# Backward pass of attention and a gated MLP: P and dS kept in pairs of row tiles, and one transposing DMA a pair

## The chip, the cores and the metric

The kernel runs on one core of a Trainium2 chip. A core has TensorE (PE in the profile; PEld is its weight load), VectorE (DVE), ScalarE (ACT), GpSimd (POOL) and SyncE (SP), an on-chip memory of 128 partitions (SBUF), matmul accumulators (PSUM), and 16 DMA engines that serve all its queues. Here SP issues DMAs on the hardware queue (q1 in the profile), POOL on the software queue (q0). The metric is device time in microseconds (us), the median of several runs.

## What is computed

The reference is a block whose output is `x + s * g`, and the gradients of it for nine outputs. With `xn` the layer norm of `x` (2048 rows, 576 columns):

```python
q = (xn @ wq)                      # 32 heads of 128
p = softmax(q @ k.T * Dh ** -0.5)  # 2048 x 2048 in each head
s = (p @ v) @ wo
h = sigmoid(xn @ w_gate) * (xn @ w_up)   # 4608 columns
g = silu(h @ w_down)
out = x + s * g
```

The kernel returns `out` and the gradients for x, the K and V caches, wq, wo, w_gate, w_up and w_down. K and V are given as caches of 32 heads, 2048 keys, 128 columns; all is bf16. For one head the backward pass needs P and dS = P * (dP - delta), both 2048 x 2048, in two forms: as they are, with queries on partitions, as the moving operand of dV = P^T dO and dK = dS^T Q; and turned, with keys on partitions, as the stationary operand of O = P V and dQ = dS K.

## The kernel before

**Stages.** (1) The gated MLP forward and its row-wise results, to 460 us of the profiled execution. (2) The 32 heads, one after the other with an overlap, 460 to 3670 us. (3) Output rows and the gradient that goes into the MLP (3670 to 3800). (4) A loop over 18 blocks of 256 MLP columns (F blocks) that makes dh, dw_down, dw_up and dw_gate (3800 to 4410). (5) dwo and dwq by groups of four heads (4410 to 4660). (6) dx by blocks of 256 rows (to the end).

**A head.** NT = 16 row tiles of 128 queries. `s_half` (L544) makes half a row of scores (two matmuls of 512 columns) and DVE scales it and takes its running minimum; `s_exp` (L558) makes the row tile P(q) of 128 x 2048 on ACT; `dp_half` (L573) makes dP and, on DVE and ACT, the row tile dS(q). Each P(q) and dS(q) is a buffer of 512 KB in the pool `slab` (20 buffers). `trans_dma` (L599) issues from SP a transposing DMA that turns one row tile into 16 blocks of 128 x 128 in the pool `wpt` (7 buffers). One row tile, dS(9), is turned on PE instead (`trans_pe`, L602, over `pe_transposes`, L515: eight 128 x 128 transposes into a PSUM bank, then a copy by ACT or DVE, twice). `rows` and `row_mm` (L608) then multiply the turned tile by V or K, 16 matmuls of 128 columns a row tile, four row tiles to an accumulator; `o_sink` (L650) and `dq_sink` (L670) take the results away. `kv` and `kv_mm` (L626, L635) make dV and dK from the slabs as they are, in two passes each (VA, VB, KA, KB), and store them transposed (dvT_d, dkT_d).

**Order.** PE, DVE and ACT run the heads in an order written out by hand: each piece of work has a position, 64 a head, and the program is sorted by it (`at`, `anchor`, L442). Scores of row tile q stand at 2q and 2q + 1, dP at 32 + 2q and on; O starts at `XO`, dQ at 32 + `XQ`; the matmuls of dV and dK fill from `KV0` to `KV1`, spread by `level` so that each position holds the same load. Work of the next head (Q, K, V preparations) has positions in this one. SP and POOL are not in that order: a scheduler sets theirs, and each runs in order once it is set. SP issues all transposes of a head. A transpose waits for its row tile and for its `wpt` buffer.

**Turning back.** dvT_d and dkT_d have to be turned into the output's form: 64 transposes of 512 KB (HBM to SBUF, `turn`, L151) and 64 writes, all on SP. `turn(pool, n)` first writes what the call before loaded, then loads n more. It is called once in each F block (n = 2, 36 in all), once a group in stage 5 (n = 2, 16 in all) and in stage 6 (n = 1, the last 12). In an F block SP also loads the a and b blocks of the block after next (`load_abh`, L878) and a piece of w_down, turned (`load_wdT`, L836). SP's order in stages 3 to 6 is that of the program text.

## Time and profile before

| | us |
|---|---|
| median of 3 runs (lowest, highest) | 5088.66 (5080.39, 5103.23) |
| profiled execution: its time, its span | 5100.3, 5098.5 |
| PE busy in the span | 4977.9 (98%) |
| DVE, ACT, POOL busy | 3087.7, 2435.7, 1484.0 |
| heads, stage 2 | 460 to 3670 |
| granted PE clock (mean) | 0.994 |
| P turned by DMA: 512, median from issue to landing | 5.8 |
| dS turned by DMA: 480, median from issue to landing | 5.9 |

The page gives busy time by engine, a timeline in 40 slices, the DMA queues with the share of the span that their packets took, the chain of work that ended last, and the costliest groups of instructions with the idle time before them and what ended it. SPq is SP's own queue: a DMA's duration there is the time that SP was held by its issue, waits included, and not the time to its landing. As packets overlap, the shares of the queues can sum to over 100%. A matmul's duration holds its way through the array; back to back, a 128-column one starts every 0.056 us.

### The profile page before, as it was taken

How to read it: one execution, taken by the hardware profiler on the slowest of the kernel's cores; microseconds unless marked ns; L12 is line 12 of the kernel's file. 1: busy time of each engine (PE TensorE's matmuls, PEld its weight loads, DVE VectorE, ACT ScalarE, POOL GpSimd, SP SyncE). 2: the span in 40 equal slices, each digit the busy share in tenths (PEclk: the TensorE clock that was granted, in tenths of full speed). 3: DMA queues.
4: the chain of work that ended last, by engine and by line, in shares of the span. 5: the costliest groups of instructions: out<-in, count | busy, mean ns of one | idle time of the engine just before them, and what ended most of it. 6: DMA issues, size and time to landing. Idle time of an engine off the chain costs nothing.

```text
span 5098.5 us, 103815 instructions
## 1 busy us (share of the span) xinstructions
PE 4977.9 (98%) x43024; PEld 3071.8 (60%) x43024; DVE 3087.7 (61%) x4821; ACT 2435.7 (48%) x3131; POOL 1484.0 (29%) x2197
## 2 busy tenths in 40 slices
PE   9999999999999999999999999999899999899999
PEld 3344666666666666666666666666457777654554
DVE  6556778878887887887888788777432222110101
ACT  5533656666666676666666667666202122100000
POOL 4322323333333333233333323322223223211000
PEclk9999999999999999999999999999999999999999
DMA  7889999999999999999999999999999999999995
GB/s 260 265 206 167 197 198 201 198 197 200 202 200 203 203 201 204 202 203 202 199 200 200 205 204 197 199 199 203 189 235 262 230 244 252 282 278 254 207 198 119
DMA packets 2855051, 1079.04 MB, mean 212 GB/s; under 512 B 2659889, under 2 KB 2782769, under 8 KB 2854577
## 3 DMA queue, kind: packets, MB, share of 16 engines
q1 hardware_dynamic: 2769312, 786.61, 87.3%
q0 software_dynamic: 85264, 285.79, 19.8%
q8 instruction: 336, 5.51, 0.4%
q14 instruction: 139, 1.13, 0.1%
HBM read 172.54 MB, written 234.55 MB: 80 GB/s over the span
## 4 chain that ended last, share of the span: by engine, by line
PE 86%; DMA 8%; issue 2%; DVE 2%; ACT 1%; POOL 1%; SPq 0%; DVEq 0%; POOLq 0%; ACTq 0%
PE acc L612 16%; PE acckv L630 15%; PE sp L552 8%; PE acc L1072 8%; PE dp L582 7%; PE accp L511 5%; PE accw L947 4%; DMA dST<-dSq 4%; PE dh L905 3%; PE acc L392 3%; PE accd L923 3%; PE acc L1005 3%; PE acc L852 2%; PE accq L1014 2%; PE acct L518 2%
## 5 line engine op out<-in xcount | busy, mean ns | idle before, releaser
L563 ACT ACTIVATE Pq<-sneg,nm 128x2048 bf16<-128x2048 bf16 x512 | 1025.0, 2002 | 182.6 <-DVE sneg L554 181.6
L585 DVE SCALAR_TENSOR_TENSOR dSq<-dp,delta,Pq 128x1024 bf16<-128x1024 f32 x608 | 774.9, 1282 | 445.9 <-PE dp L582 442.9
L612 PE MATMUL acc<-Kn,dST 128*128 128x128 bf16 x8192 | 977.0, 219 | 36.9 <-DMA dST<-dSq 36.2
L612 PEld LDWEIGHTS <-dST 128*128 128x128 bf16 x8192 | 692.3, 98 | 464.7 <-DMA dST<-dSq 57.6
L612 PE MATMUL acc<-Vn,PT 128*128 128x128 bf16 x8192 | 948.8, 219 | 11.7 <-DMA PT<-Pq 11.6
L612 PEld LDWEIGHTS <-PT 128*128 128x128 bf16 x8192 | 682.7, 98 | 428.8 <-DMA PT<-Pq 18.6
L630 PE MATMUL acckv<-Pq,dOn 128*128 128x512 bf16 x2048 | 762.9, 380 | 0.0
L630 PE MATMUL acckv<-dSq,Qn 128*128 128x512 bf16 x2048 | 758.9, 379 | 0.0
L554 DVE TENSOR_SCALAR_CACHE_REDUCE sneg<-sp,nm 128x1024 bf16<-128x1024 f32 x512 | 657.0, 1283 | 97.6 <-PE sp L552 64.8
L554 DVE TENSOR_SCALAR_CACHE_REDUCE sneg<-sp 128x1024 bf16<-128x1024 f32 x512 | 625.2, 1221 | 92.2 <-PE sp L552 82.8
L588 ACT ACTIVATE t<-dp,negdelta 128x1024 bf16<-128x1024 f32 x416 | 464.8, 1117 | 426.0 <-PE dp L582 324.5
L552 PE MATMUL sp<-KT,QT 128*128 128x512 bf16 x2048 | 610.5, 380 | 7.3 <-DVE sneg L554 7.0
L582 PE MATMUL dp<-VT,dOT 128*128 128x512 bf16 x2048 | 609.9, 379 | 0.6 <-DVE dSq L585 0.5
L592 DVE TENSOR_TENSOR dSq<-t,Pq 128x1024 bf16<-128x1024 bf16 x416 | 307.3, 739 | 0.0
L571 POOL TENSOR_TENSOR dOn<-dOn,rinv_all 128x256 bf16<-128x256 bf16 x256 | 153.8, 610 | 491.6 <-DVE dOn L42 305.4
L630 PEld LDWEIGHTS <-dOn 128*128 128x128 bf16 x2048 | 200.5, 98 | 74.5 <-issue 0.4
L630 PEld LDWEIGHTS <-Qn 128*128 128x128 bf16 x2048 | 200.5, 98 | 73.8
L511 PE MATMUL accp<-xnT,wq_h 128*128 128x512 bf16 x640 | 240.9, 381 | 2.8 <-ACT xnT L40 0.8
L947 PEld LDWEIGHTS <-xn_all 128*128 128x128 bf16 x2304 | 224.2, 98 | 27.8
L1085 DVE SCALAR_TENSOR_TENSOR junk<-dxn,xn_all 128x576 f32<-128x576 f32 x16 | 12.1, 758 | 369.3 <-ACT dxn L1080 369.3
L676 POOL DMA_DIRECT2D dq_d<-dq_n x128 | 99.1, 774 | 456.6 <-DVE dq_n L675 419.4
L1072 PEld LDWEIGHTS <-cf 128*128 128x128 bf16 x2304 | 146.3, 98 | 141.3 <-DMA cf<-dg_d 3.8
(186 smaller groups left out, 7059.2 us busy)
## 6 DMA issues: line engine op xcount, KB each, us to landing
out_dram<-turn SPq DMA_DIRECT2D x64, 512.0 KB, 4.9
h_d<-h_row POOLq DMA_DIRECT2D x48, 384.0 KB, 3.0
a_d<-a_row POOLq DMA_DIRECT2D x48, 384.0 KB, 3.5
b_d<-b_row POOLq DMA_DIRECT2D x48, 384.0 KB, 4.5
a_blk<-a_d SPq DMA_DIRECT2D x18, 1024.0 KB, 8.3
b_blk<-b_d SPq DMA_DIRECT2D x18, 1024.0 KB, 21.4
du_d<-du_blk POOLq DMA_DIRECT2D x18, 1024.0 KB, 9.6
dg_d<-dg_blk POOLq DMA_DIRECT2D x18, 1024.0 KB, 12.5
```

The source lines that it names most:

```text
L511: nc.tensor.matmul(acc[:], lhsT=w[:, i, :], rhs=(srcT if i < DL else xnT)[:, i, cs], start=(i == 0), stop=(i == DL))
L552: nc.tensor.matmul(sp[:, c * CH:(c + 1) * CH], lhsT=hs.QT[:, qs], rhs=hs.KT[:, hf * HW_ + c * CH: hf * HW_ + (c + 1) * CH], start=True, st ...
L554: nc.vector.tensor_scalar(sneg[:, hf * HW_:(hf + 1) * HW_], sp[:], -SCALE, None if hf == 0 else nm[:, hf - 1:hf], op0=ALU.mult, op1=ALU.mi ...
L563: nc.scalar.activation(Pq[:], sneg[:], AF.Exp, bias=nm[:, hf:hf + 1], scale=-1.0, accum_out=hs.rs_all[:, qt:qt + 1])
L582: nc.tensor.matmul(dp[:, c * CH:(c + 1) * CH], lhsT=hs.dOT[:, qs], rhs=hs.VT[:, hf * HW_ + c * CH: hf * HW_ + (c + 1) * CH], start=True, s ...
L585: nc.vector.scalar_tensor_tensor(dSq[:, hsl], dp[:], hs.delta[:, qt:qt + 1], Pq[:, hsl], op0=ALU.subtract, op1=ALU.mult)
L588: nc.scalar.activation(t[:], dp[:], AF.Identity, bias=hs.negdelta[:, qt:qt + 1], scale=1.0)
L592: nc.vector.tensor_tensor(dSq[:, hsl], t[:], Pq[:, hsl], op=ALU.mult)
L612: nc.tensor.matmul(bx.acc[:, j, :], lhsT=T[qt][:, kt, :], rhs=getattr(hs, rhs)[:, kt, :], start=(kt == 0), stop=(kt == NT - 1))
L630: nc.tensor.matmul(bx.acc[i][:], lhsT=getattr(hs, rhs)[:, qt, :], rhs=slabs[qt][:, k0:k0 + CH], start=(qt == 0), stop=(qt == NT - 1))
L947: nc.tensor.matmul(acc[:kd, :FB], lhsT=xn_all[:, st, d0:d0 + kd], rhs=blk_[:, st, :], start=(st == 0), stop=(st == NT - 1))
L1072: nc.tensor.matmul(accs[sl][j][:, :nn], lhsT=ch[:, kk, sl * P:(sl + 1) * P], rhs=w_[:, n0:n0 + nn], start=(pi == 0 and kk == 0), stop=(las ...
```

## The change

P and dS of two neighbouring row tiles now lie in one slab buffer (`[P, 2, S]`, 10 buffers), and one transposing DMA from SP turns both into 32 blocks of 128 x 128 (`trans_P`, `trans_dS`; `wpt` has 4 buffers of two row tiles). It is issued after the second row tile. dS(9) goes by DMA as well, and `trans_pe` is gone, with its load in the planner. O and dQ start 1.5 positions later (`XO`, `XQ` 12.1 to 13.6), and the positions of the preparations, of dV and dK are set anew. The scaling of Q by the softmax's denominators is a step of its own (`q_scale`). To fit, `wq_h` and `ou` have one buffer instead of two, and the stores of dV, dK and dQ share three. `turn` loads at most one, before it writes the older ones; it is called 27 times in the F blocks (once in each, and once more at the start of every odd one, with three buffers), 16 in stage 5 (twice a group), 21 in stage 6. In the F blocks `load_wdT` now stands ahead of `load_abh`.

```diff
...
-    def turn(pool, n):
-        while turned:
-            nc.sync.dma_start(*turned.pop(0))
-        for _ in range(n):
-            if turns:
-                src, dst = turns.pop(0)
-                t_ = pool.tile([P, NT, P], bf, name="turn")
-                nc.sync.dma_start_transpose(t_[:], src)
-                turned.append((dst, t_[:]))
+    def turn(pool, load=True):
+        old, turned[:] = list(turned), []
+        if load and turns:
+            src, dst = turns.pop(0)
+            t_ = pool.tile([P, NT, P], bf, name="turn")
+            nc.sync.dma_start_transpose(t_[:], src)
+            turned.append((dst, t_[:]))
+        for (dst, t_) in old:
+            nc.sync.dma_start(dst, t_)
...
     KPC = CH // P
-    NSLAB, NPT = 20, 7
+    NSLAB, NPT = 10, 4
     STT2 = {4, 9, 14}
-    PE_P = set()
-    PE_DS = {9}
     with tc.tile_pool(name="ld2", bufs=2) as ld2, tc.tile_pool(name="ld1q", bufs=1) as ld1q, \
...
                 self.t_ = {}
+                self.Pp = {}
+                self.dSp = {}
                 self.dS = [None] * NT
...
             hc = slice(hs.h * P, (hs.h + 1) * P)
-            hs.wq = wh.tile([P, DT, P], bf, name="wq_h")
+            hs.wq = wh.tile([P, DT, P], bf, name="wq_h", bufs=1)
             nc.gpsimd.dma_start(hs.wq[:, :DL, :], A_wq[:DL * P, hc].rearrange("(t p) c -> p t c", p=P))
...
             pe_transposes(lambda j: hs.QT[:, j * P:(j + 1) * P], hs.Qn, g, eng)
+        def q_scale(hs, g):
             gs = slice(g * 8, (g + 1) * 8)
...
             hf = NHF - 1
-            Pq = slabp.tile([P, S], bf, name="Pq", tag="slab")
-            hs.P[qt] = Pq
-            nc.scalar.activation(Pq[:], sneg[:], AF.Exp, bias=nm[:, hf:hf + 1], scale=-1.0, accum_out=hs.rs_all[:, qt:qt + 1])
+            if qt % 2 == 0:
+                hs.Pp[qt] = slabp.tile([P, 2, S], bf, name="Pq", tag="slab")
+            Pq = hs.P[qt] = hs.Pp[qt - qt % 2][:, qt % 2, :]
+            nc.scalar.activation(Pq, sneg[:], AF.Exp, bias=nm[:, hf:hf + 1], scale=-1.0, accum_out=hs.rs_all[:, qt:qt + 1])
...
             if hf == 0:
-                hs.dS[qt] = slabp.tile([P, S], bf, name="dSq", tag="slab")
+                if qt % 2 == 0:
+                    hs.dSp[qt] = slabp.tile([P, 2, S], bf, name="dSq", tag="slab")
+                hs.dS[qt] = hs.dSp[qt - qt % 2][:, qt % 2, :]
             dSq = hs.dS[qt]
...
-        def t_tile(T, qt, name):
-            if T[qt] is None:
-                T[qt] = wpt.tile([P, NT, P], bf, name=name, tag="PT")
-            return T[qt]
-        def trans_dma(T, slabs, qt, name):
-            nc.sync.dma_start_transpose(t_tile(T, qt, name)[:], slabs[qt][:])
-        def trans_pe(T, slabs, qt, name, g, eng):
-            pe_transposes(lambda j: slabs[qt][:, j * P:(j + 1) * P], t_tile(T, qt, name), g, eng)
+        def trans_dma(T, pair, qt, name):
+            t_ = wpt.tile([P, 2 * NT, P], bf, name=name, tag="PT")
+            nc.sync.dma_start_transpose(t_[:], pair[:].rearrange("p a s -> p (a s)"))
+            for j in range(2):
+                T[qt + j] = t_[:, j * NT:(j + 1) * NT, :]
+        def trans_P(hs, qt):
+            trans_dma(hs.PT, hs.Pp.pop(qt), qt, "PT")
+        def trans_dS(hs, qt):
+            trans_dma(hs.dST, hs.dSp.pop(qt), qt, "dST")
...
                 c = half * 2 + i
-                kv_t = stg.tile([P, CH], bf, name="kv")
+                kv_t = stg.tile([P, CH], bf, name="kv", tag="stg", bufs=3)
                 alt.copy(kv_t[:], acc[:], eng=KVE[i])
...
             def sink(acc):
-                bx.ou = wt.tile([P, GQ, P], bf, name="ou")
+                bx.ou = wt.tile([P, GQ, P], bf, name="ou", bufs=1)
                 alt.copy(bx.ou[:], acc[:], eng=OUE)
...
             def sink(acc):
-                dq_n = stg.tile([P, GQ, P], bf, name="dq_n")
+                dq_n = stg.tile([P, GQ, P], bf, name="dq_n", tag="stg", bufs=3)
                 nc.vector.tensor_tensor(dq_n[:], acc[:], bcast(hs.rsc[:, gs], GQ), op=ALU.mult)
...
         HEAD = 2 * H1
-        XO, XQ = 12.1, 12.1
+        XO, XQ = 13.6, 13.6
         KVE, OUE = "ss", "s"
-        WOT_AT, DST_PE = 2.0, (6.3, 8.2)
-        QT_AT, DOT_AT = ((41.4, 46.7, 50.0, 53.8), "s"), ((5.6, 8.6, 13.4, 17.4), "s")
-        KT_AT, DON_AT, VT_AT, QN_AT = (45.5, 49.2, "s"), (16.2, 25.4, "v"), (29.6, 31.2, "s"), (33.6, 39.4, "s")
+        WOT_AT = 1.6
+        QT_AT, DOT_AT = ((39.0, 47.2, 50.2, 56.4), "s"), ((7.8, 10.4, 16.2, 18.6), "s")
+        KT_AT, DON_AT, VT_AT, QN_AT = (42.0, 43.6, "s"), (14.9, 24.4, "v"), (3.4, 26.4, "s"), (28.0, 32.2, "s")
         PSTEP = 0.4
...
-        KV0, KV1, GAP = 24.0, 86.7, 1.1
+        KV0, KV1, GAP = 23.2, 85.9, 1.1
         BLK, WIDE = 1.0, CH / P
...
             load_[int(p_)] += DT
-        for ps_, n_ in [((KT_AT + DON_AT + VT_AT + QN_AT), 8), ([H1 + 2 * q_ + d_ for q_ in PE_DS for d_ in DST_PE], 8)]:
+        for ps_, n_ in [((KT_AT + DON_AT + VT_AT + QN_AT), 8)]:
             for p_ in ps_:
...
                 if len(out) < n and len(out) % (2 * KPC) == 0:
-                    pos = max(pos, 4.0 * (len(out) // (4 * KPC)) + 8.0)
+                    pos = max(pos, 4.0 * (len(out) // (4 * KPC)) + 7.0)
             return out, pos
...
                 at(b + QN_AT[g], prep_qn, hs, g, QN_AT[2])
+                at(b + max(QN_AT[g] + 0.3, 16 * g + 14.2 + RINV_AT), q_scale, hs, g)
             for p in range(NT // 2):
...
                 at(p1 + EXP_AT, s_exp, hs, qt)
-                if qt in PE_P:
-                    for g in range(2):
-                        at(p1 + 5.3 + g, trans_pe, hs.PT, hs.P, qt, "PT", g, "s")
-                else:
-                    at(p1 + PT_AT, trans_dma, hs.PT, hs.P, qt, "PT")
-                if qt in PE_DS:
-                    for g in range(2):
-                        at(p2 + DST_PE[g], trans_pe, hs.dST, hs.dS, qt, "dST", g, "sv"[g])
-                else:
-                    at(p2 + DST_AT, trans_dma, hs.dST, hs.dS, qt, "dST")
+                if qt % 2:
+                    at(p1 + PT_AT, trans_P, hs, qt - 1)
+                    at(p2 + DST_AT, trans_dS, hs, qt - 1)
             for g in range(NG):
...
         FB = min(256, F)
-        with tc.tile_pool(name="b1o", bufs=2, reuse_waits="tile") as outp, tc.tile_pool(name="b1k", bufs=2, reuse_waits="tile") as tkp, tc.tile_pool(name="b1t", bufs=3, reuse_waits="tile") as tmpp, \
+        with tc.tile_pool(name="b1o", bufs=2, reuse_waits="tile") as outp, tc.tile_pool(name="b1k", bufs=3, reuse_waits="tile") as tkp, tc.tile_pool(name="b1t", bufs=3, reuse_waits="tile") as tmpp, \
                 tc.tile_pool(name="b1r", bufs=2, reuse_waits="tile") as dblk, \
...
             for fb in range(F // FB):
+                if fb % 2:
+                    turn(tkp)
                 fcols = slice(fb * FB, (fb + 1) * FB)
...
                         make_dwd(fl)
-                load_abh(fb + 2)
                 if fb < DT * (NWD - 1):
                     load_wdT(fb % DT, 1 + fb // DT)
-                turn(tkp, 2)
+                load_abh(fb + 2)
+                turn(tkp)
                 for (blk_, out_, nm) in ((du_blk, out_7, "dwu"), (dg_blk, out_6, "dwg")):
...
                     nc.gpsimd.dma_start(out_[D - KL:, fcols], dwl[k * KL:(k + 1) * KL, :])
-            turn(tkp, 0)
+            turn(tkp, False)
         pcw.release()
...
                                              start=(st == 0), stop=(st == NT - 1))
+                    if hl == 0:
+                        turn(tkp)
                     dwo = sb.tile([P, D], bf, name="dwo")
...
                     nc.sync.dma_start_transpose(dst[:, :, d0:d0 + kd], src[d0:d0 + kd, :])
-                turn(tkp, 2)
-            turn(tkp, 0)
+                turn(tkp)
+            turn(tkp, False)
...
                     elif sbi and pi % 3 == 1:
-                        turn(tkp, 1)
+                        turn(tkp)
                     last = pi == len(passes) - 1
...
                     (nc.sync if sbi == NSB - 1 else nc.gpsimd).dma_start(o1[rows, :], dx[:])
-            turn(tkp, 0)
+            turn(tkp, False)
             assert not turns
...
```

## The prediction

> **What bounds the kernel now.** I read the page's first part, then busy time by stage, then who PE waits for, then DMA and SP's queue over one head. Over the span TensorE (PE) is 98% busy and the hardware DMA queue 87%:
> ```profile
> PE 4977.9 (98%) x43024; PEld 3071.8 (60%) x43024; DVE 3087.7 (61%) x4821; ACT 2435.7 (48%) x3131; POOL 1484.0 (29%) x2197
> ...
> q1 hardware_dynamic: 2769312, 786.61, 87.3%
> ```
> Heads 1 to 30 (560 to 3530 us; the second column is the stretch, the third PE's busy time), and what PE waits for there (us in all, times, longest):
> ```profile
> 560.00:3530.00 2970.00, 2941.27 (x26825) 1870.99 (x26823) 2385.27 (x3453) 1944.47 (x2221) 989.78 (x1405) 1.00 1.14 201
> ...
> PE acc L612 <- DMA dST<-dSq: 19.4, 23, 1.9
> PE acc L612 <- DMA PT<-Pq: 3.4, 5, 1.8
> ```
> All but 6 of PE's 29 idle us there are waits for a row tile that a transposing DMA has not turned yet. DVE is 80% busy, ACT 65%: neither bounds. The first score matmul of head 1 starts at 563.98, that of head 31 at 3530.25: 98.9 us a head; a head without a wait takes 97.87 (1557.75 to 1655.62, head 11). Positions below are 64ths of a head, 1.53 us.
>
> One head (1459 to 1557 us) by DMA queue, and SP's own queue over it (start, duration, count):
> ```profile
> q1 hardware_dynamic: 62576, 15.78, 99.4%
> q0 software_dynamic: 1161, 3.39, 13.1%
> ...
> 1467.34 50.15 SPq L600 DMA_TRANSPOSE PT<-Pq  x16
> 1517.59 44.45 SPq L600 DMA_TRANSPOSE dST<-dSq  x13
> ```
> The reader is to see that SP issues one transpose behind the other without a gap: 16 in 50.15 us, 3.13 each, while PE makes a row tile every two positions (3.06). In this head P(7) is ready at 27.1 us from its first score matmul, its transpose begins at 31.8 and lands at 36.7, PE uses it at 40.2. So the transposing queue is a second bound, level with PE. Taking plain traffic off at its own share (13.1% of 97.9 = 12.8 us), 31 transposes share 85.1 us: 2.74 each.
>
> After the heads PE loses time in a few gaps (3800 to 4430 us):
> ```profile
> PE acc L1005 <- DMA onb<-on_d: 13.0, 1, 13.0
> PE dh L905 <- ACT dhc L909: 8.6, 3, 7.7
> PE dh L905 <- DMA wdT<-in_B_w_down_dram: 7.9, 1, 7.9
> ```
>
> **The change part by part.** The sum is made against the profiled execution: 5100.3 us (span 5098.5), 11.6 above the median of the three runs, 5088.66.
>
> *Removed: PE's turning of dS(9).* 16 transposes a head, 512 in all. In the chain eight take 0.45 us, 0.056 each:
> ```profile
> 1498.24 0.45 PE acct L518 x8
> ```
> 512 x 0.056 = 28.8 us, on the engine that is 99% busy: **-28.8**, and an undisturbed head becomes 97.0. With them go 32 evictions on ACT (1.00 us) and 32 on DVE (0.68); both engines have over 19% idle: 0.
>
> *Added and merged: DMA transposes.* 31 a head of 512 KB become 16 of 1 MB; the bytes turned rise by 1/31. The trace has no 1 MB transpose out of SBUF. The nearest row has the same size, queue and engines, but reads HBM (last stage, two of them):
> ```profile
> 4959.69 9.61 SPq L1061 DMA_TRANSPOSE cq<-dq_d  x2
> ```
> 4.8 us each. The other end is two singles, 2 x 2.74 = 5.48. A head's DMA time would be 12.8 + 16 x 4.8 = 89.6, or 12.8 + 16 x 5.48 = 100.5; PE's 97.0 is reached at 5.26 a pair. I take 5.0 (nearer to the row of the same size, with some surcharge for plain traffic that stops a longer DMA as well): 92.8, so PE sets the head and the queue gets 4 us of slack that it hasn't now. By that most waits go; I keep 9 of the 22.8 us, since longer DMAs come in coarser steps: **-14**. Ends: no wait left, -23; a DMA-bound head of 100.5, (100.5 - 98.9) x 31 = +50 in place of -28.8 and -14.
>
> [...] The rows first: a cf transpose (24 blocks of 128x128) takes 3.4 us on SP's queue, cq (32) 4.8, wqT (8) 1.3: 0.14 to 0.16 a block at any length. [...]
>
> *Later and coarser.* A pair goes out when its second tile is ready. P(7) was ready 27.1 us after the start, 3.7 positions behind its slot (14), so pair k is ready at 4k + 5.7 and O uses it from 4k + 13.6: 7.9 positions, 12.1 us. A 1 MB transpose lands 7.3 us after issue (cq's median), so a backlog of 4.8 us is borne; before it was 8.4 positions, 12.8 us, less 5.8 = 7.0. dS has some 9 positions, 13.7 us, less 7.3 = 6.4. The margin is thinner; that it holds hangs on the queue's slack. If it is gone, PE stands still with kv, score and dP matmuls behind it in its written order, and DVE and ACT wait in turn.
>
> *Buffers.* Four pairs of turned tiles for seven singles: pair k+4 is wanted at 4k + 20.7, buffer k is free at 4k + 17.6, 3 positions before (2.6 before the change). Slabs: from the written positions the tightest are dS pair 2, wanted at 40.0, freed by the second dV pass at 38.3 (dS(4) had 1.3 positions): 0. One wq buffer: free when Q's projection ends at 58.0, next read at 39.0 a head later: its load waits in POOL's queue, behind it dq writes that nobody waits for soon: 0. One ou, three shared stg tiles: at most three are written together (dV's last two and a dQ, near 53): 0 to +3 in all, taken 0.
>
> *Retuned positions* (Q, dO, K, V preparations, dV/dK from 23.2 to 85.9): same instructions, PE work moved inside a head: 0, ends -5 and +10, seen only where a head has no fill. Splitting q_scale off moves POOL work (1.9 us each) that POOL, 33% busy, hides.
>
> *Head 31 and the tail.* SP's order keeps an oT transpose ahead of the last dS. Now:
> ```profile
> 3652.19 7.48 SPq L600 DMA_TRANSPOSE dST<-dSq  x1
> ```
> PE waits 12.7 us for it. Then the last pair waits there: one more tile to turn (2.4) and 16 more matmuls after it (0.9): **+3**, ends 0 and +6.
>
> *turn().* In the F-block loop SP carried two turns per block and waited 109 us for their writes, since a turn needs a buffer whose write was issued just ahead. Now 27 turns (not 36), three buffers, the transpose ahead of the older write, wdT ahead of the a/b loads. The 7.9 us for wdT should go: it was issued at 3982, behind two turns of 13 and 17 us, and now leaves a block earlier. The 7.7 us (b_blk landed 3 us after the loop wanted it) should mostly go, but wdT's 8 to 18 us on SP now stand ahead of the a/b loads: **-11**, ends -15.6 and +8. The 13 us at the next stage end with onb, whose issue waits for PE's last accw of the loop: **-2** (less traffic beside it), ends -6 and +2. Nine more turns go to the last stage, where the DMA share is 0.62 in the last 148 us: hidden. But the last one's write now stands behind the last dx write on SP (5095.6); a turn's write lands 2.8 to 4.9 us after issue, dx's landed 1.8 after: **+2**, ends +1 and +4.
>
> Sum: -28.8 - 14 + 3 - 11 - 2 + 2 = -50.8: 5049 in an execution like the profiled one; less 11.6, **5038** as a median, said 5040.
>
> **The rivals.**
> 1. *Pairs cost as much as two singles, and the transposing queue bounds the head (slower).* One mechanism: at more than 5.26 us a pair 16 pairs and plain traffic pass PE's 97.0; at 5.48 a head takes 100.5. For it: SP's queue never stands still now, a 32nd tile is added, the price looks like one per block. Against: cq's 4.8, and between two singles there is a new start of the queue each time. Heads +50, the rest -8: 5088.7 + 42 = 5131. It ends slower from about 5.4 a pair on.
> 2. *The queue stays level with PE* (5.2 to 5.35 a pair): the 28.8 us are given back as waits at L612; heads -5, the rest -8: 5076, inside the half per cent.
> 3. *All waits go*: pairs at 4.8, no stall, both loop gaps closed: -28.8 - 23 + 1 - 15.6 - 6 + 1 = -71: 5017. For it: 8 us of slack a head.
>
> **How the numbers follow.** Half a per cent (25 us) is about what a measurement of this kernel can tell from no change: the three runs before span 23 us. Chances: forecast 0.46, rival 3 0.20, rival 2 0.15, rival 1 0.19. Faster by over 0.5% (under 5063): 0.66; within: 0.15; slower: 0.19. The forecast's own range with rival 3 is 5005 to 5062; to leave out no more than 2 in 10 it has to reach into rival 1: 5005 to 5125, as the DMA's price is open from both sides.
>
> **What would show it.** Right: dST and PT about 5 us each on SP's queue with gaps between them, so that SP waits for data; PE's period near 97.0 a head; waits at L612 under 10 us in heads 1 to 30; no acct from dSq; no wait for wdT. Wrong: SP's queue again without gaps and 16 pairs in over 84 us, waits for dST in the hundreds of ns in every head (rival 2) or 2 us and more (rival 1); a new wait of dh for b_blk; DVE or ACT waiting for slabs; a longer end than 3 us behind the last dx.

## The result, and the profile after

The changed kernel takes 5139.77 us (median of 11 runs; 5112.70 to 5157.23) against 5102.59 us for the kernel before, run beside it. The ratio is 1.0065, with a 95% interval of 1.0038 to 1.0091: slower by 0.65%, where the forecast was 5040 us and faster. The profiled execution spans 5154.8 us, 56.3 more than the one of before.

Stage by stage, in the two profiled executions (each stage runs from its first instruction to the next stage's first; the heads are counted from each head's first exponential on ACT):

| stage | before, us | after, us | difference |
|---|---|---|---|
| up to head 1 | 568.8 | 578.6 | +9.8, of which 9.3 lie before the first score matmul (470.1 to 479.4) |
| heads 1 to 30 | 2966.3 | 2996.0 | +29.7 |
| head 31 and the last dQ | 135.0 | 128.0 | -7.0 |
| output rows | 131.4 | 142.1 | +10.7 |
| F blocks, with the wait before dw | 621.0 | 621.9 | +0.9 |
| dw | 253.4 | 258.1 | +4.7 |
| dx | 422.6 | 429.9 | +7.3 |

Two of these differences should not be read as the change's alone: the first and the output rows. Three of the kernels below (e1_lag8, m_turnold, g4_qs) are the same as the changed one up to the first score matmul and start it at 468 to 469 us; the granted clock up to head 1 was 0.985 to 0.988 in them and 0.979 here. The output rows take 135.8 to 146.6 us in the twelve profiles with pairs and 131.4, 135.7 and 137.8 in the three with singles, so the kernel before had the shortest of all; what the change adds there was not taken apart. The profiled execution of the changed kernel (5156.55 us) is also one of its slowest: by the medians the loss is 37 us and not 56.

In the heads PE's work did shrink: an average head took 98.88 us with 0.80 of PE waits before, and 99.87 with 2.66 after, so 98.08 and 97.21 without them. The waits took it back. First, who PE waits for in heads 1 to 30 of the changed kernel (us in all, times, longest):

```profile
PE acckv L635 <- POOL dOn L573: 22.2, 30, 0.8
PE acckv L635 <- ACT kv L40: 21.4, 30, 0.7
PE acc L617 <- ACT dOT L40: 15.0, 30, 0.8
PE acct L517 <- ACT VT L40: 11.7, 30, 0.5
PE acc L617 <- DMA dST<-dSq: 5.8, 4, 3.2
```

The reader is to see the column of counts. The waits for turned tiles, 22.8 us before, are down to 5.8 in 4 places. Four others stand 30 times each, once in every head, at the same place (a fifth, for KT's copy, 30 times 0.12 us, lies below what this view lists). A wait that occurs in every head at the same place points to the written order and not to chance on the queue; the experiments test that.

SyncE's queue over head 11 (start, duration, count) holds 8 pairs in 48.69 us, 6.09 each with the waits for their data in it, where the forecast had 5 us each and gaps between them.

```profile
1582.22 48.69 SPq L600 DMA_TRANSPOSE PT<-Pq  x8
1631.01 44.00 SPq L600 DMA_TRANSPOSE dST<-dSq  x7
```

What has changed is how far it runs behind: before, a transpose began on average 1.6 to 8.4 us after its tile was ready (by the tile's place in the head), now 0.1 to 2.0 us.

After the heads, the wait for wdT and the 13.0 us for onb are gone, and in their place stand five for dhc, ACT's copy of dh (3840 to 4480 us):

```profile
PE dh L906 <- ACT dhc L910: 22.7, 5, 9.7
PE accd L924 <- DMA h_blk<-h_d: 3.1, 1, 3.1
```

How one of these comes about is seen on SyncE's queue (start, duration; PE's wait of 8.1 us ends at 3967.7):

```profile
3921.15 16.67 SPq L156 DMA_TRANSPOSE turn<-dvT_d  x1
3939.18 0.36 SPq L159 DMA_DIRECT2D out_dram<-turn  x1
3939.59 2.18 SPq L836 DMA_TRANSPOSE wdT<-in_B_w_down_dram  x1
3941.86 0.56 SPq L884 DMA_DIRECT2D a_blk<-a_d  x1
3942.51 14.70 SPq L884 DMA_DIRECT2D b_blk<-b_d  x1
```

The turn holds the queue 16.67 us, a_blk can only be issued at 3941.86 and lands at 3962.48, b_blk at 3966.40; VectorE's products with them (du_blk waits 8.1 us for a_blk, then dg_blk 3.5 for b_blk) hold dhc, and dhc holds PE. The chain that ended last is 68% "DMA b_blk<-b_d" over the 35 us from 3940 to 3975.

### The profile page after: what moved, and what is told of

Read it like the earlier page. It is cut to its first block, busy times and chain, and to the rows that moved or that the text cites. A ratio compares the mean times of both kernels' runs of the same rounds, so it can differ in the third digit from the quotient of the medians.

```text
span 5154.8 us, 100626 instructions
## 1 busy us (share of the span) xinstructions
PE 4926.1 (96%) x41765; PEld 3051.4 (59%) x42512; DVE 3157.1 (61%) x4789; ACT 2415.2 (47%) x3099; POOL 1479.5 (29%) x2197
## 3 DMA queue, kind: packets, MB, share of 16 engines
q14 instruction: 127, 1.04, 0.1%
## 4 chain that ended last, share of the span: by engine, by line
PE 76%; DMA 7%; issue 6%; DVE 5%; ACT 5%; POOL 1%; SPq 1%; ACTq 0%; DVEq 0%; POOLq 0%; another core or an unknown queue 0%
PE acc L617 14%; PE acckv L635 13%; PE acc L1075 8%; PE dp L586 7%; PE sp L553 6%; PE accp L510 5%; PE accw L948 4%; DVE sneg L555 3%; PE acc L391 3%; PE dh L906 2%; PE accd L924 2%; PE acc L1006 2%; PE accq L1017 2%; DMA b_blk<-b_d 2%; PE acc L851 2%
## 5 line engine op out<-in xcount | busy, mean ns | idle before, releaser
L617 PE MATMUL acc<-Kn,dST 128*128 128x128 bf16 x8192 | 1034.5, 219 | 28.3 <-DMA dST<-dSq 16.7
L589 DVE SCALAR_TENSOR_TENSOR dSq<-dp,delta,Pq 128x1024 bf16<-128x1024 f32 x608 | 773.2, 1281 | 378.8 <-PE dp L586 377.2
L617 PEld LDWEIGHTS <-dST 128*128 128x128 bf16 x8192 | 713.8, 98 | 466.8 <-issue 28.0
L635 PE MATMUL acckv<-dSq,Qn 128*128 128x512 bf16 x1915 | 707.5, 380 | 23.1 <-ACT kv L40 22.1
L635 PE MATMUL acckv<-Pq,dOn 128*128 128x512 bf16 x1892 | 701.0, 380 | 26.5 <-POOL dOn L573 22.8
L553 PE MATMUL sp<-KT,QT 128*128 128x512 bf16 x1985 | 597.9, 380 | 7.0 <-DVE sneg L555 6.7
L586 PE MATMUL dp<-VT,dOT 128*128 128x512 bf16 x1913 | 580.4, 379 | 1.8 <-DVE dSq L589 1.0
L596 DVE TENSOR_TENSOR dSq<-t,Pq 128x1024 bf16<-128x1024 bf16 x416 | 407.4, 979 | 0.0
L1088 DVE SCALAR_TENSOR_TENSOR junk<-dxn,xn_all 128x576 f32<-128x576 f32 x16 | 12.1, 758 | 381.3 <-ACT dxn L1083 381.3
L1083 ACT ACTIVATE dxn<-acc 128x512 f32<-128x512 f32 (+1 forms) x32 | 12.8, 406 | 413.6 <-issue 344.3
## 6 DMA issues: line engine op xcount, KB each, us to landing
dg_d<-dg_blk POOLq DMA_DIRECT2D x18, 1024.0 KB, 12.8
```

The source lines that it names most:

```text
L553: nc.tensor.matmul(sp[:, c * CH:(c + 1) * CH], lhsT=hs.QT[:, qs], rhs=hs.KT[:, hf * HW_ + c * CH: hf * HW_ + (c + 1) * CH], start=True, st ...
L586: nc.tensor.matmul(dp[:, c * CH:(c + 1) * CH], lhsT=hs.dOT[:, qs], rhs=hs.VT[:, hf * HW_ + c * CH: hf * HW_ + (c + 1) * CH], start=True, s ...
L589: nc.vector.scalar_tensor_tensor(dSq[:, hsl], dp[:], hs.delta[:, qt:qt + 1], Pq[:, hsl], op0=ALU.subtract, op1=ALU.mult)
L596: nc.vector.tensor_tensor(dSq[:, hsl], t[:], Pq[:, hsl], op=ALU.mult)
L617: nc.tensor.matmul(bx.acc[:, j, :], lhsT=T[qt][:, kt, :], rhs=getattr(hs, rhs)[:, kt, :], start=(kt == 0), stop=(kt == NT - 1))
L635: nc.tensor.matmul(bx.acc[i][:], lhsT=getattr(hs, rhs)[:, qt, :], rhs=slabs[qt][:, k0:k0 + CH], start=(qt == 0), stop=(qt == NT - 1))
```

## The experiments

The theory that the traces suggested: the pairs do what was forecast, and the loss is made by the retuned positions (the waits above, some 2.5 us a head). Rival A: the pairs themselves cost it. Rival B: the turn part makes it. Each kernel below was run beside the kernel before on the same chip, and its ratio is to that.

### One constant of the planner put back (e1_lag8)

```
-                    pos = max(pos, 4.0 * (len(out) // (4 * KPC)) + 7.0)
+                    pos = max(pos, 4.0 * (len(out) // (4 * KPC)) + 8.0)
```

> The changed kernel with the planner's floor put back from 7.0 to 8.0 and nothing else. Theory (the retuned positions cost: VA's last row tiles now come ahead of the last dOn scaling, 0.74 us of PE wait in each of the 30 heads, 22.2 us of the 79.7 us that PE waits there): the wait of accumulation VA for dOn goes, but VB then lets go of the first pair of P later and the slab of dS pair 2 comes later, so a new wait of the dP/dS work may take part of it: heads 1 to 30 fall by 0 to 22 us, total 5110 to 5140 us. Rival A (pairs themselves cost, positions do not): the wait only changes its name, heads stay at 99.9 us each. Rival B (the turn part costs): unchanged within noise.

Measured: 5124.34 us, ratio 1.0050 (1.0021 to 1.0079). Heads 1 to 30: 2975.8 us, 20.2 less than the changed kernel. PE's waits there:

```profile
PE dp L586 <- ACT t L592: 16.6, 30, 0.6
PE acc L617 <- DMA dST<-dSq: 14.2, 11, 3.0
PE dp L586 <- DVE dSq L589: 9.1, 30, 0.5
```

The wait for dOn is gone, and so, by the shift of everything behind it, are those for the copies of kv and dOT. A new one has come, 0.85 us a head of the dP products: with a floor of 8.0 the second dV pass lets go of the first pair of P 0.7 positions after dS pair 2 wants that slab (worked out from the written positions; 1.7 ahead with 7.0). So 7.0 bought the slab in time, and paid with dOn. The place of the new wait fits that; no run isolates it. The heads fell within the theory's 0 to 22 us; the timed gain alone, 1.0065 to 1.0050, is inside the intervals.

### All positions of before, the later rows kept (e2_oldpos)

```
-        QT_AT, DOT_AT = ((39.0, 47.2, 50.2, 56.4), "s"), ((7.8, 10.4, 16.2, 18.6), "s")
+        QT_AT, DOT_AT = ((41.4, 46.7, 50.0, 53.8), "s"), ((5.6, 8.6, 13.4, 17.4), "s")
...
-        KV0, KV1, GAP = 23.2, 85.9, 1.1
+        KV0, KV1, GAP = 24.0, 86.7, 1.1
```

> The changed kernel with all of the positions of before (weights, QT, dOT, KT, dOn, VT, Qn, start of KV streams, floor 8.0); pairs, the later O and dQ rows and the turn part stay. Theory (positions cost about 2.5 us a head): the five waits that stand in every head (dOn 0.74, kv copy 0.71, dOT copy 0.50, VT copy 0.39, KT copy 0.12 us) go, heads 1 to 30 at about 97.5 us each instead of 99.87, so 60 to 75 us less: about 5070 us; if the slab of dS pair 2 is then waited for, 0.5 to 1 us of it comes back per head. Rival A (pairs cost the time): heads stay at 99 to 100 us, total 5120 to 5150 us. Rival B (turn part): heads may fall, the stages behind the heads keep the 10 us more of the output rows.

Measured: 5353.67 us, ratio 1.0510 (1.0449 to 1.0571). A plain miss: 106.44 us a head, not 97.5. Waits in heads 1 to 30:

```profile
PE accp L510 <- DVE dq_n L680: 54.3, 30, 1.8
PE acckv L635 <- ACT kv L40: 51.5, 30, 1.7
PE acckv L635 <- POOL dOn L573: 46.3, 30, 1.5
PE acc L617 <- DVE dq_n L680: 40.0, 30, 1.3
```

Again each stands in every head (another, for ou's copy, 38.8 us, twice), and most are for evictions. Projections, turnings, O and dQ rows and the two KV accumulations share four accumulators of PSUM; with rows at 13.6 and the rest where it was, an accumulator is asked for while its last result is still being copied out. The positions are not 32 free numbers but one arrangement: the later rows need other places for the rest.

### The pairs in the old order altogether (e5_oldrows)

```
 (e2_oldpos, and)
-        XO, XQ = 13.6, 13.6
+        XO, XQ = 12.1, 12.1
```

> The changed kernel with all positions of before, the O and dQ rows at 12.1 too, so the pairs alone in the old order. Tells whether the 13.6 of the rows or the pairs made e2_oldpos 250 us slower. Theory (the rows at 13.6 collided with the old positions of the projections and turnings, which share four accumulators of PSUM): the 5 waits of e2_oldpos for dq_n, kv, ou and dOn go, and in their place waits for PT and dST come back, since a pair lands later than a single and the rows have 1.5 positions (2.3 us) less margin: 40 to 100 us of PE waits in the heads, 98.5 to 101 us a head, total 5110 to 5190 us. Rival A (pairs break the old order by themselves): it stays near 106 us a head.

Measured, in a single execution: 5134.44 us, 99.97 us a head. All five waits of e2_oldpos are gone, and these remain:

```profile
PE acc L617 <- DMA PT<-Pq: 41.3, 60, 2.5
PE acc L617 <- DMA dST<-dSq: 32.5, 40, 2.5
```

As expected: pairs turned and used in the old order come too late for the rows by up to 2.5 us, 74 us in all. This is what the move of the rows to 13.6 removes, and that move in turn forces the retuning, which cost about as much.

### Singles for all 32 tiles (e4_singles32)

```
-    PE_DS = {9}
+    PE_DS = set()
```

> The kernel before with dS row tile 9 turned by DMA too, so 32 single transposing DMAs a head and none on PE; no pairs. Prediction's rival 1 priced this: 32 x 2.74 us = 87.7 us and the row loads' share on the queue, and the queue of SyncE leads the heads. Theory: SyncE's transposes become the bound or go later still, PE waits for dST and PT grow from 23 us in the heads to 60 us or more, while PE's own work falls by 0.96 us a head: total 5100 to 5160 us. If the queue has room (Rival A in its strict form, pairs give nothing over singles): total about 5070 us.

Measured: 5186.27 us, ratio 1.0197 (1.0138 to 1.0256), above the range given. Heads at 102.06 us, PE waiting (heads 1 to 30):

```profile
PE acc L612 <- DMA PT<-Pq: 68.4, 51, 6.0
PE acc L612 <- DMA dST<-dSq: 50.1, 61, 2.3
```

So 32 singles bind the head at about 102 us. The pairs of e5_oldrows carry the same bytes in the same order of the heads: 99.97 us a head, with 73.8 us of waits where the singles have 118.5. A pair is cheaper than two singles, and the prediction's first rival falls. Of rival A a part stays: in the old order the heads with pairs are longer than those of the kernel before (99.97 against 98.88 us), as a pair lands too late there. In an order that fits them, heads of 97.1 us are reached (g3_best, below).

### The turn part alone, and the rest alone (e3_turn, m_turnold)

e3_turn is the kernel before with the changed `turn()`, its calls, the third buffer and the order of loads. m_turnold is the changed kernel with these as before.

```
 e3_turn, on the kernel before (m_turnold undoes the same on the changed kernel)
-    def turn(pool, n):
+    def turn(pool, load=True):
...
-    tc.tile_pool(name="b1k", bufs=2, ...)
+    tc.tile_pool(name="b1k", bufs=3, ...)
...
+                if fb % 2:
+                    turn(tkp)
...
-                load_abh(fb + 2)
                 if fb < DT * (NWD - 1):
                     load_wdT(fb % DT, 1 + fb // DT)
-                turn(tkp, 2)
+                load_abh(fb + 2)
+                turn(tkp)
...
                         (dw)
+                    if hl == 0:
+                        turn(tkp)
...
-                turn(tkp, 2)
+                turn(tkp)
```

> The kernel before with the turn part of the change alone (three-buffer pool in the F blocks, one turn at each call, order of loads). The heads are those of before. The prediction's terms for this part sum to -11 us: expected 5090 us by them, with output rows 131, F blocks 610, dw 253, dx 423 us. Theory: no gain and no loss, as the changed kernel's F blocks kept 622 us, 5090 to 5115 us. Rival B: the late stages are 10 to 20 us longer as in the changed kernel (output rows 142, dw 258, dx 430 us): 5115 to 5125 us.

> The changed kernel with the turn part of before. Rival B: dx at 423 instead of 430 us, dw 254 instead of 258 us: 5125 to 5135 us. Theory: heads stay at 99.87 us; if the turn part is neutral 5140 us.

Measured: e3_turn 5116.64 us, ratio 1.0042 (1.0007 to 1.0076); m_turnold 5121.16 us, ratio 1.0020 (0.9987 to 1.0054). So the turn part alone costs 0.42%, and without it the change costs 0.20% and not 0.65%: 0.45% by the mirror. A third pair below (f1_pos and f2_pos_late) gives 0.46%. One such contrast is hardly outside its interval; three that agree are. It is about 22 us, where the prediction had -11.

Where they lie is seen from PE's gaps of over 0.25 us in the late stages, averaged over the profiles of kernels with the changed turn part (after, e1, e2, e3, e5, f1, g4_qs, and g2_dw but for dx) and with that of before (before, e4, m_turnold, f2, g1_a, g1_b, g3_best):

| PE's gaps, us | turn of before, mean (range) | changed turn, mean (range) |
|---|---|---|
| F blocks | 9.7 (1.1 to 20.3) | 24.7 (6.9 to 38.8) |
| before dw, and in it | 9.4 (0.0 to 15.9) | 1.8 (0.0 to 7.3) |
| dx | 5.8 (3.7 to 8.6) | 12.1 (9.2 to 17.7) |

The wait before dw went, as the new order of loads would have it, and twice that came in the F blocks, whose ranges overlap; dx lost 6 us, and its ranges don't. That makes 14 of the 22 us. By the lengths of the stages the same profiles differ by 11.4 us in the F blocks with the wait before dw, 2.7 in dw and 6.7 in dx, 20.8 together. The gaps are not all of it: in the F blocks the granted clock was 0.982 in the mean with the changed turn part and 0.994 with that of before; whether a lower clock follows the gaps or comes beside them no run shows.

What stands before dx on SyncE's queue in e3_turn, whose dx begins on PE at 4715.4:

```profile
4689.10 1.91 SPq L156 DMA_TRANSPOSE turn<-dkT_d  x1
4691.05 0.58 SPq L159 DMA_DIRECT2D out_dram<-turn  x1
4694.77 2.57 SPq L156 DMA_TRANSPOSE turn<-dvT_d  x1
4697.77 0.34 SPq L159 DMA_DIRECT2D out_dram<-turn  x1
4702.31 2.23 SPq L156 DMA_TRANSPOSE turn<-dkT_d  x1
4704.59 3.38 SPq L159 DMA_DIRECT2D out_dram<-turn  x2
4708.01 7.32 SPq L1064 DMA_TRANSPOSE cf<-du_d  x2
```

In these rows the queue issues in the order of the program text, one DMA behind the other. Each turn needs one of two buffers, so it stands until the write just ahead of it has landed (the write of 4691.05 lands at 4694.70, the next turn starts at 4694.77), and the first cf of dx is issued only 7.3 us ahead of PE's first product with it (15.8 us ahead in the kernel before).

### Two turns taken out of that chain (g2_dw)

```
 (f1_pos, and)
                     if hl == 0:
-                        turn(tkp)
+                        turn(tkp, hg < NHG - 1)
...
-                turn(tkp)
+                turn(tkp, hg < NHG - 1)
...
-                    elif sbi and pi % 3 == 1:
+                    elif sbi and (pi % 3 == 1 or (sbi < 3 and pi == 5)):
                         turn(tkp)
```

> The kernel of f1_pos (turn part of the change) without the two turns of dw's last group of heads, which two passes of dx take instead. Tells whether the chain of turns that stands in front of the first transposing loads of dx on SyncE's queue makes dx 6 us longer. If so, the first cf load is issued 12 us or more ahead of its first product instead of 7 to 10, the first waits of dx for cf (9 to 18 us in the five kernels with the turn part, 6 in the four without) fall to 6 us, and dx from 428 to 422 to 425 us. If not: dx stays at 428 us and more.

Measured, in a single execution (5092.61 us): the first cf is issued 18.4 us ahead of its product, dx takes 423.5 us (f1_pos 428.3) with gaps of 5.3 us. PE's waits for cf<-du_d in the first 100 us of dx, 6.9 us in the changed kernel and 4.4 in f1_pos, are gone; 3.9 for cf<-dg_d and 1.4 for cq stay. It is one execution, but its dx lies among those with the turn part of before (420.7 to 425.5 us) and outside those with the changed one (428.3 to 431.9). So this part of the loss is the chain of turns in front of dx.

### Four positions moved by half a position or less (f1_pos, f2_pos_late)

```
-        QT_AT, DOT_AT = ((39.0, 47.2, 50.2, 56.4), "s"), ((7.8, 10.4, 16.2, 18.6), "s")
+        QT_AT, DOT_AT = ((39.0, 47.2, 50.2, 56.4), "s"), ((7.8, 10.4, 16.0, 18.4), "s")
...
-        ... VT_AT ... (3.4, 26.4, "s")
+        ... VT_AT ... (3.4, 25.9, "s")
-        KV0, KV1, GAP = 23.2, 85.9, 1.1
+        KV0, KV1, GAP = 23.2, 86.3, 1.1
-                    pos = max(pos, 4.0 * (len(out) // (4 * KPC)) + 7.0)
+                    pos = max(pos, 4.0 * (len(out) // (4 * KPC)) + 7.5)
```

Why half a position matters is seen on ACT in the changed kernel (head 12; start, duration):

```profile
1703.84 2.00 ACT L565 ACTIVATE Pq<-sneg,nm 128x2048 bf16<-128x2048 bf16 x1 [0.82 <-DVE sneg L555]
1705.74 0.19 ACT L565 ACTIVATION_READ_ACCUMULATOR Pq<-sneg,nm 128x1 f32 x1
1705.84 0.56 ACT L40 CAST dOT<-accp 128x512 bf16<-128x512 f32 x1
```

The last dOT projection ends at position 20.2, an exponential stands in ACT's order at 20.1. Its copy therefore comes behind 2.0 us of exponential, and PE's next O group, which wants that accumulator, starts at 1706.45. PE's row there:

```profile
1706.45 0.38 PE L617 MATMUL acc<-Vn,PT 128*128 128x128 bf16 x4 [0.49 <-ACT dOT L40]
```

Ending at 20.0, as in these two kernels, the projection's copy comes ahead of the exponential, and the wait for dOT, 15.0 us in the changed kernel, is not in f1_pos's view below.

> The changed kernel with four positions moved by half a position or less and nothing else: floor 7.0 to 7.5, the last two dOT projections 16.2 and 18.6 to 16.0 and 18.4, the second VT 26.4 to 25.9, end of the KV streams 85.9 to 86.3. Each is aimed at one wait that stood in all 30 heads: dOn (22.2 us), dOT copy (15.0), VT copy (11.7), kv copy (21.4). Theory (the pairs did what was forecast, and the waits come from where the positions fall against the exponentials on ACT and the scaling on POOL): these 70 us fall to under 25, heads 1 to 30 from 99.87 to 97.6 to 98.3 us each, total 5070 to 5095 us, against before 0 to 35 us faster. Rival A (waits move elsewhere, the work of pairs paces the heads): heads stay above 99 us, total 5115 us or more.

> The kernel of f1_pos with the turn part of before: dV and dK turned in pairs of loads and writes in the F blocks and in dw as before, two buffers. Theory as for f1_pos in the heads. Rival B (the turn part costs, seen in e3_turn as the first cf transpose of dx issued 48 us later on SyncE's queue): dx goes from 430 to 423 us, dw from 258 to 254 us, 5 to 15 us less than f1_pos: 5055 to 5085 us, 20 to 45 us faster than before. If the turn part is neutral: the same as f1_pos within 5 us.

Measured: f1_pos 5117.06 us, ratio 1.0012 (0.9984 to 1.0039); f2_pos_late 5086.43 us, ratio 0.9966 (0.9929 to 1.0003). Against the changed kernel (1.0065) and m_turnold (1.0020) the four moves give 0.53 and 0.54%. Waits in heads 1 to 30 of f1_pos:

```profile
PE acc L617 <- DMA dST<-dSq: 24.1, 16, 3.0
PE acct L517 <- DVE dOn L42: 16.0, 28, 0.6
PE acckv L635 <- POOL dOn L573: 12.2, 30, 0.4
PE acc L617 <- DMA PT<-Pq: 6.2, 8, 2.2
```

Of the 70 us aimed at, 12.2 are left. But VT, moved forward, now waits for the eviction of dOn ahead of it, and the waits for turned tiles, 5.8 us in the changed kernel, are 30 again, in single heads. An undisturbed head takes 98.1 us; the mean is 99.33, above the 97.6 to 98.3 expected. The theory held for the waits, not for the mean, and the total is in rival A's range (5115 us or more): once PE stands still less, it runs into the transposing queue. f2_pos_late just misses its range of 5055 to 5085 us; its dx, 423.9 us, came as expected.

### Two attempts at the rest (g1_a, g1_b)

```
 g1_a, on f2_pos_late
-        KT_AT, DON_AT, ... = (42.0, 43.6, "s"), (14.9, 24.4, "v"), ...
+        KT_AT, DON_AT, ... = (42.0, 43.8, "s"), (14.9, 24.0, "v"), ...
-        KV0, KV1, GAP = 23.2, 86.3, 1.1
+        KV0, KV1, GAP = 23.2, 86.3, 0.9
-                    pos = max(pos, 4.0 * (len(out) // (4 * KPC)) + 7.5)
+                    pos = max(pos, 4.0 * (len(out) // (4 * KPC)) + 7.8)
 g1_b: the same KT, dOn and 7.8, and
-    STT2 = {4, 9, 14}
+    STT2 = {3, 9, 14}
-        KV0, KV1, GAP = 23.2, 86.3, 1.1
+        KV0, KV1, GAP = 23.2, 85.9, 1.1
```

> The kernel of f2_pos_late (pairs, turn part of before) with the two waits that were left in every head aimed at: floor 7.5 to 7.8 (dOn scaling, 0.41 us a head), second dOn turning 24.4 to 24.0 (0.54 us a head ahead of VT), second KT turning 43.6 to 43.8 (0.12), gap between the KV streams 1.1 to 0.9 so that VB still lets go of the first pair of P in time. Theory: an undisturbed head goes from 98.1 to 97.0 to 97.3 us (before 97.9); disturbed heads, where a transposing DMA lands late, stay. Heads 1 to 30 at 98.0 to 98.8 us in the mean, total 5045 to 5075 us, ratio to before 0.990 to 0.995. If the transposing queue is the next bound (its DMAs hold SyncE 95 us a head in f2_pos_late), the waits for PT and dST grow by what the others lose, the heads stay at 99.2 us and the total at 5086 us.

> As g1_a, but the gap of 1.1 is kept and the slab of dS pair 2 is given one position in another way: row tile 3 instead of 4 takes the short path on VectorE, so that pair 2 is first written by the second half of tile 4. Theory: the same 97.0 to 97.3 us an undisturbed head. If the slab binds: waits of the dP products for dS of 0.5 to 1 us a head as in e1_lag8, 98 us. If the transposing queue binds: no gain over f2_pos_late.

Measured: g1_a 5087.06 us, ratio 0.9977 (0.9952 to 1.0002), heads at 98.9 us undisturbed; g1_b 5177.61 us, ratio 1.0153 (1.0111 to 1.0195), most heads at 102.0. Both miss. Turning dOn earlier did not bring its eviction earlier, because that stands behind a score eviction in VectorE's order; PE only came to the wait sooner (26.4 us now). And with tile 3 in place of 4 on the short path, PE waits 2 us a head for VectorE:

```profile
PE dp L587 <- DVE dSq L590: 61.4, 30, 2.2
```

Why tile 4 was a good place is not settled by this run; tiles 1 and 2 are the slow ones on VectorE (next), and tile 3 comes right behind them.

### The scaling of Qn, on VectorE and later (g4_qs)

```
         def q_scale(hs, g):
             gs = slice(g * 8, (g + 1) * 8)
+            eng = nc.vector if g else nc.gpsimd
-            nc.gpsimd.tensor_scalar(...)       (and tensor_tensor)
+            eng.tensor_scalar(...)             (and tensor_tensor)
...
-                at(b + max(QN_AT[g] + 0.3, 16 * g + 14.2 + RINV_AT), q_scale, hs, g)
+                at(b + (28.3, 42.3)[g], q_scale, hs, g)
```

> The changed kernel with one step moved: the scaling of the second half of Qn goes from GpSimd at 34.8 to VectorE at 42.3. In the changed kernel that scaling (1.90 us on GpSimd) runs beside two products of dS on VectorE, which take 2.18 and 2.88 us there instead of 0.68 (before: 1.23 and 0.89). Theory (these two are off the path that sets the end; PE's four waits per head are of other origin): the two products fall to 0.7 to 1.2 us, VectorE's mean of that group from 979 to 750 ns, and the heads stay within 0.5 us of 99.87, total within 0.3% of the changed kernel's 5140 us. Rival (VectorE's delay is what makes the last dOn scaling late, since its reciprocal queues behind those products): PE's wait for dOn (22.2 us) falls too, heads at 99.1 to 99.4 us, total 5115 to 5128 us.

Measured: 5138.30 us, ratio 1.0038 (1.0008 to 1.0069); the interval takes in the changed kernel's 1.0065. The profiled heads take 99.77 us and the undisturbed ones 99.6 as before the edit, the wait for dOn is still 18.7 us in 30 places (22.2 before the edit, but 18.7 in m_turnold too, without it). The first of the two slow products is back at 0.68 us; the second still takes 2.87, which the theory had not expected. On the path of the heads neither shows, as the theory had it.

### The waits removed at their source (g3_best)

```
 (m_turnold and g4_qs, and)
                 for p in range(NT // 2):
+                    r_ = 3.05 if p == NT // 2 - 1 else RINV_AT
-                    at(b + 4 * p + 2 + RINV_AT, s_rinv, hs, p)
-                    at(b + max(4 * p + 2.1 + RINV_AT, DON_AT[p // 4] + 0.5), s_scale, hs, p)
+                    at(b + 4 * p + 2 + r_, s_rinv, hs, p)
+                    at(b + max(4 * p + 2.02 + r_, DON_AT[p // 4] + 0.5), s_scale, hs, p)
...
-        ... DOT_AT = ..., ((7.8, 10.4, 16.2, 18.6), "s")
+        ... DOT_AT = ..., ((7.8, 10.4, 16.0, 18.4), "s")
-        ... VT_AT ... (3.4, 26.4, "s")
+        ... VT_AT ... (3.4, 26.4, "v")
-        KV0, KV1, GAP = 23.2, 85.9, 1.1
+        KV0, KV1, GAP = 23.2, 86.3, 1.3
-                    pos = max(pos, 4.0 * (len(out) // (4 * KPC)) + 7.0)
+                    pos = max(pos, 4.0 * (len(out) // (4 * KPC)) + 7.2)
```

The last dOn scaling was late since its reciprocal stood in VectorE's order behind the delta of an O group. In the changed kernel (VectorE, then GpSimd; start, duration):

```profile
1725.94 0.68 DVE L668 TENSOR_REDUCE delta<-prod 128x4 f32<-128x512 f32 x1
1726.54 0.15 DVE L569 RECIPROCAL rinv_all<-rs_all 128x2 f32<-128x2 f32 x1
```

```profile
1726.72 0.22 POOL L669 TENSOR_SCALAR negdelta<-delta 128x4 f32<-128x4 f32 x1 [2.53 <-DVE rinv_all L569]
1726.91 0.60 POOL L573 TENSOR_TENSOR dOn<-dOn,rinv_all 128x256 bf16<-128x256 bf16 x1
```

> Pairs with the turn part of before, and each wait that stood in every head removed at its source: the last reciprocal and dOn scaling ahead of the delta of O group 1 (34.6 to 33.05), floor 7.2, gap of the KV streams 1.3, last dOT projections 16.0 and 18.4, VT's eviction on VectorE instead of ACT at 26.4, Qn scaling as in g4_qs. Theory: the waits that stand in every head fall from 2.2 to 2.7 us to under 0.6, an undisturbed head 97.0 to 97.5 us, heads 1 to 30 at 97.8 to 98.6 in the mean, total 5050 to 5080 us, ratio to before 0.990 to 0.995. Rival (the transposing queue is the next bound: it holds SyncE 95 us a head and its idle time fell from 7.0 us a head in the changed kernel to 3.8 in f2_pos_late): an undisturbed head does fall to 97.5, but waits for PT and dST take 1 us and more a head, mean 98.8 to 99.3 us, total 5075 to 5095 us, no faster than f2_pos_late.

Measured: 5059.13 us against 5113.26 for the kernel before beside it, ratio 0.9901 (0.9868 to 0.9934): 1% faster. Heads 1 to 30 take 2945.6 us, 98.19 each; an undisturbed head 97.10, with 0.2 us of waits. One such, by busy time (stretch, its length, PE's busy time and count), and all waits of heads 1 to 30 that reach this view:

```profile
1652.32:1749.42 97.10, 96.87 (x879) 61.52 (x877) 81.91 (x119) 61.97 (x72) 30.70 (x45) 1.00 1.17 207
```

```profile
PE acc L619 <- DMA dST<-dSq: 20.1, 20, 2.9
PE acc L619 <- DMA PT<-Pq: 5.5, 9, 1.2
```

Nothing of the written order is left. What remains, 25.6 us, is what the kernel before had, 22.8 us for the same two: single heads in which a pair lands late. SyncE's queue is idle 3.5 us a head here, 7.0 in the changed kernel and 3.6 in the kernel before. So both readings of this run's expectation are partly right: the gain is there, and the transposing queue is again the next bound. In total the run is inside the theory's range. Against m_turnold (1.0020), which differs from it in the positions and the Qn scaling alone, it is 1.2% faster.

## Why the prediction was wrong, point by point

**PE's turning of dS(9), -28.8: right.** An undisturbed head goes from 97.87 us to 97.10 with 0.2 of waits in it, so 0.97 less work, against the 0.96 of the forecast.

**Pairs by DMA, 5.0 us each between 4.8 and 5.48: right in kind, too low in size.** Singles bind the head at 102.06 us, pairs let 97.1 through, so 16 pairs fit into it with the plain traffic; estimated with the forecast's own share for that traffic, a pair costs (97.1 - 12.8) / 16 = 5.27 at most. By the same estimate two singles cost more here: (102.06 - 12.8) / 16 = 5.58. So the longer instruction saved something. But a pair holds SyncE's queue for 5.49 us (PT) and 5.95 (dST) in the median, waits for data included, and PT lands 8.6 us after its issue and not 7.3. The 4 us of slack a head that the forecast added for the queue did not come: it is idle 3.5 us a head in g3_best and 3.6 in the kernel before.

**Waits, -14: right in the changed kernel by accident.** They fell from 22.8 to 5.8 us. But g3_best, with no other waits, has 25.6. What gave the queue its slack in the changed kernel was largely the 2.5 us a head for which PE stood still elsewhere (queue idle 7.0 us a head there, 3.5 in g3_best). The term should have been near 0: that is the mechanism of the prediction's second rival, a queue level with PE, behind waits that hid it.

**The margin of the rows: right.** e5_oldrows shows what happens without the 1.5 positions (74 us of waits); with them 5.8 us are left in the changed kernel.

**Buffers, 0: right, but with a bill elsewhere.** dS pair 2's slab did come in time. It came in time because the planner's floor had been lowered to 7.0, and that floor put the last dV matmuls ahead of the last dOn scaling.

**Retuned positions, "same instructions, PE work moved inside a head: 0, ends -5 and +10": this step failed.** It is +74: 22.2 for dOn, 21.4 for kv, 15.0 for dOT, 11.7 for VT and 3.6 for KT, each 30 times. The step counted instructions and not the order on the other engines. Here an eviction's place against ACT's 2.0 us exponential, or a scaling's against VectorE's delta, decided whether PE could go on, and each miss was paid in every head. The prediction bounded that at 10 us without a row. It could have been worked out: the last dOT step at 20.2 beside an exponential at 20.1, VT at 26.4 beside one at 26.1, dOn's scaling for the last pair at 34.7 beside its use at 35.0 are all in the written positions.

**Head 31 and the tail, +3: wrong in sign.** 135.0 to 128.0 us; PE waits 10.9 us for turned dS there, 4.6 at the longest, where it waited 16.9 with one of 12.7. A transpose of oT still stands ahead of the last dS, but it holds the queue 5.51 us and the pair behind it 5.27, where it was 7.22 and 7.48 for a single tile; why they were shorter is open.

**turn(), -11, -2 and +2: this step failed too.** About +22 by three timed contrasts, which is also the larger part of the loss by the clock (0.45 of 0.65%). The waits that it named did go (wdT's 7.9, onb's 13.0 entirely). But the end given as bad, +8, "wdT's 8 to 18 us on SP now stand ahead of the a/b loads", was too small, and in the row shown it is not wdT that stands there for long (2.18 us) but the turn ahead of it (16.67). And the turns were priced as hidden by their share of DMA, not by their place on a queue that issues in order: PE's gaps in dx grew by 6.3 us, most of it by that (g2_dw takes 4.8 us off dx). The last write came as forecast, 1.3 us behind dx's (forecast 2).

In the profiled heads the sum is therefore -26 (work) - 17 (waits for turned tiles) + 74 (positions), about the +29.7 measured. None of the three rivals was this. The one that ended slower had the wrong mechanism: it lost the time to pairs as dear as two singles. Taken apart by the timed ratios, the 0.65% are a gain of 1.0% (g3_best against the kernel before), a loss of 1.2% by the positions (m_turnold against g3_best) and one of 0.45% by the turn part (the changed kernel against m_turnold). (The "8 us of slack a head" of the third rival is 97.0 - 89.6 = 7.4 in the prediction's own numbers.)

## What to carry to other kernels

When an order written out by hand is shifted, lay each eviction's place against the long instructions of the engine that makes it, and against its next user, before costing the shift at nothing: a wait that stands once in a loop's body is paid in every turn of it. Here waits that occurred as often as the loop turns came from the order, and waits for turned tiles in single heads from the queue; the count column is a first hint. It isn't proof: in e5_oldrows the waits for PT stand 60 times, twice a head, as the rows there come too early for the pairs. And a change of several parts is best taken apart on the chip: here the pairs in a fitting order were worth 1%, hidden under positions that cost 1.2% and a turn part that cost half a per cent.

## What the runs showed of the hardware

One group on VectorE went from 739 to 979 ns though its operation did not change (kernel before, then after):

```profile
L592 DVE TENSOR_TENSOR dSq<-t,Pq 128x1024 bf16<-128x1024 bf16 x416 | 307.3, 739 | 0.0
```

```profile
L596 DVE TENSOR_TENSOR dSq<-t,Pq 128x1024 bf16<-128x1024 bf16 x416 | 407.4, 979 | 0.0
```

All of it is in two of the 13 products of a head, 2.18 and 2.88 us in the median, where the kernel before has 1.23 and 0.89; the other eleven take 0.68 in both. Around them in the changed kernel (VectorE, then GpSimd):

```profile
1728.18 2.18 DVE L596 TENSOR_TENSOR dSq<-t,Pq 128x1024 bf16<-128x1024 bf16 x1
1730.40 1.28 DVE L589 SCALAR_TENSOR_TENSOR dSq<-dp,delta,Pq 128x1024 bf16<-128x1024 f32 x1
1731.60 2.88 DVE L596 TENSOR_TENSOR dSq<-t,Pq 128x1024 bf16<-128x1024 bf16 x1
```

```profile
1727.92 1.90 POOL L543 TENSOR_TENSOR Qn<-Qn,rsc 128x1024 bf16<-128x1024 bf16 x1
...
1731.76 1.17 POOL L663 TENSOR_TENSOR prod<-ou,dOn 128x512 f32<-128x512 bf16 x1
1732.88 1.04 POOL L670 TENSOR_TENSOR o_n<-ou,rinv_all 128x512 bf16<-128x512 bf16 x1
```

The slow products lie beside GpSimd's tensor products and end 0.5 us after those (1730.36 behind 1729.82, 1734.48 behind 1733.92); GpSimd's Qn scaling takes 1.90 us here and 1.89 in the mean before. VectorE's other product (L589), which reads PSUM, takes 1.27 to 1.29 us in all 608 places of the run, also beside such work: 1.28 at 1746.43, where o_n runs on GpSimd from 1746.02 (1.04). g4_qs took the Qn scaling away and the first product fell to 0.68, the second, beside prod and o_n, stayed at 2.87. Beside GpSimd, then, the second product took 2.88 us and not 0.68, a little over four times its time, while prod and o_n took 1.17 and 1.04, their medians over the run. It is not always VectorE that is longer: prod at 1744.70, begun while such a product ran (1744.37, 0.68), takes 1.36, and the product keeps its 0.68. Why the two engines lengthen each other's instructions no run shows.
